# Sine tables, square-root table load, last-pair casts, one stage-3 product and fillers placed elsewhere in a spectral-filter and MLP kernel

## Chip, cores, metric

One core of one Trainium2 chip. The metric is the device time of the kernel in microseconds; medians of repeated executions are given with their number.

## The reference, cut

```python
x = A_x                                             # 1 x 2048 x 512, bf16
X = rfft2(layernorm(x)) * (w_r + 1j * w_i)
h = x + irfft2(X)                                   # first half
r = relu(layernorm(h) @ w1 + b1)                    # 512 -> 1792
out = h + (r * r) @ w2 + b2                         # 1792 -> 512, second half
```

The kernel computes the transforms as matmuls with cosine and sine tables made on the chip. Frequencies are handled in eight pairs (0 to 7): stage 2 (tile U), stage 3 (X, or AB which VectorE turns into X), the product with W (mA, mB, Z, M on VectorE), stage 4 (into T2). The last stage ("s5", "s6") turns T2 into h for one of 16 row groups at a time; the MLP follows in five chunks.

## The kernel before: what the change and the argument touch

In the timelines each engine's instructions stand in the order in which the program lists them (ScalarE before: sine tables at 44.27 and 45.23 us, cast of pair 5 at 45.75, table load at 46.80, cast of pair 6 at 48.30), so an early item of a queue delays the later ones.

```python
def warm(o, n):                                     # fillers: nobody reads the result
    for _ in range(n):
        nc.tensor.matmul(o, lhsT=ones[:, 0:P], rhs=ones[:], start=True, stop=True)

ps = tc.alloc_tile_pool(name="ps", bufs=4, space=PSUM)       # 4 tiles of two banks
def mm_tile(name, dt=FP32):
    return ps.tile([P, 4096 // size(dt)], dt, tag="mm", name=name)
...
def stage4(pr, split=False):
    Z, M = Zs.pop(pr), Ms.pop(pr, None)
    pts = [mm_tile("p4a"), mm_tile("p4b")] if split else [mm_tile("p4")] * 2
    if split:                                       # pair 7
        for u, tb in (...):
            for lt in (1, 0, 3, 2):
                r, e = lt // 2, lt % 2
                nc.tensor.matmul(pts[r][:, 256 * lt:256 * lt + 256], lhsT=M[:, u, r, e::2], rhs=tb,
                                 start=(u == 0 and e == 1), stop=(u == 1 and e == 0))
    ...                                             # other pairs: one tile
    if split:
        nc.scalar.copy(dst[:, 0:2], src[0][:, 0:2])          # the two halves of T2 for pair 7
        nc.vector.tensor_copy(dst[:, 2:4], src[1][:, 2:4])
    else:
        nc.scalar.copy(dst, src[0])
...
for pr in range(9):
    if pr == 1:
        stage3(3)
    if pr + 3 < 8:
        stage2(pr + 3)
    if 1 < pr and pr + 2 < 8:
        stage3(pr + 2)
    if pr == 7:
        warm(mm_tile("idle")[:, 0:512], 3)
    if pr > 0:
        stage4(pr - 1, split=(pr == 8))
    if pr == 8:
        warm(mm_tile("idle")[:, 0:512], 3)
    if pr < 8:
        spectral(pr)                                # VectorE
    if pr == 5:
        sin_of(GI...)                               # sine tables of the last stage, ScalarE
        nc.scalar.activation(GIn..., ACT.Sin, scale=-SIN_SCALE)
    if pr == 6:
        nc.scalar.activation(junk1[:], eps[:], ACT.Sqrt, bias=eps[:])   # loads the Sqrt table
ps.release()
ps = ctx.enter_context(tc.tile_pool(name="ps2", bufs=3, space=PSUM))    # tiles of one bank
...
def s5_first(g):                                    # first products of the last stage
    two = [bank("p5o", "ph", 3), bank("p5", "pp", 3)]
    for e in range(2):                              # even l, then odd l
        for r in range(2):
            nc.tensor.matmul(two[e][:, 0:256], lhsT=T2[:, 2 * r + e, g]..., rhs=GI[:, 2 * r + e, :], ...)
...
s5_first(0); s5_whole(1); s5b(0); s6(0); s6(1)
rest = [s5(2, True), s5(3, True)]
s6a(1); s6b(0, True); s6b(1)                        # h and its statistics
warm(idle[:], 11)
...                                                 # u of groups 0 and 1, transposes, UT, MLP
```

## Time and profile before

| | before |
|---|---|
| median of the first 3 runs | 172.66 us (172.52 to 172.68) |
| span of the profiled run | 170.8 us |
| TensorE (PE) busy | 157.6 us, 92% |
| VectorE (DVE) / ScalarE (ACT) busy | 123.6 us / 106.3 us |
| granted TensorE clock (1.00 is full speed) | 1.00 |
| first MLP matmul | 56.66 us into the span |

TensorE's 92% also holds the fillers. PEld is TensorE's weight load. "idle before" stands in square brackets at the end of a timeline line, with the instruction that ended it.

### The profile page before, as it was taken

What the parts mean: (1) busy time and instruction counts of PE and PEld (TensorE: products, weight loads), DVE (VectorE), ACT (ScalarE), POOL (GpSimd) and SP (SyncE); (2) the same over time, 40 slices, a digit from 0 to 9 for tenths busy, and PEclk for the clock granted to TensorE, in tenths of its full rate; (3) what the DMA queues carried; (4) which work ended last, traced back from release to release, by engine and by line L of the source; (5) the groups of instructions that cost most, each with busy time, mean ns of one, the idle gap of its engine ahead of it and who ended that gap; (6) DMA issues with size and microseconds to landing.
All of it is one profiled execution on the core that took longest, in us unless ns stands there. A gap on an engine that the chain in (4) does not pass through costs nothing.

```text
span 170.8 us, 2709 instructions
## 1 busy us (share of the span) xinstructions
PE 157.6 (92%) x967; PEld 92.4 (54%) x981; DVE 123.6 (72%) x287; ACT 106.3 (62%) x188; POOL 36.7 (22%) x63
## 2 busy tenths in 40 slices
PE   3988797999989899899999999999999999999992
PEld 1455565887854774456445444544544454556461
DVE  6998678979956698668997577498567577578320
ACT  3999785898976772288653677245387434478200
POOL 7788900000000003134000235000034200025000
PEclk9999999999999999999999999999999999999999
DMA  5994999992000000100000100000100001010011
GB/s 165 326 281 83 223 152 272 387 241 26 0 0 0 4 0 2 55 12 0 0 31 31 35 0 2 0 31 31 35 30 0 0 31 33 25 38 0 0 60 34
DMA packets 12621, 11.42 MB, mean 67 GB/s; under 512 B 6976, under 2 KB 11072, under 8 KB 12608
## 3 DMA queue, kind: packets, MB, share of 16 engines
q1 hardware_dynamic: 12448, 10.33, 22.6%
q0 software_dynamic: 160, 0.92, 1.9%
q8 instruction: 7, 0.11, 0.3%
q14 instruction: 6, 0.05, 0.1%
HBM read 8.01 MB, written 2.10 MB: 59 GB/s over the span
## 4 chain that ended last, share of the span: by engine, by line
PE 72%; DVE 16%; ACT 5%; issue 2%; POOL 2%; DVEq 0%; POOLq 0%; ACTq 0%
PE ph L688 29%; PE po L721 25%; DVE st L215 3%; PE p L542 3%; PE p L344 3%; ACT U L361 2%; PE po L709 2%; PE p L643 2%; PE p L587 1%; PE idle L259 1%; POOL rs L222 1%; DVE KFr L226 1%; DVE mA L419 1%; ACT X L391 1%; DVE mB L419 1%
## 5 line engine op out<-in xcount | busy, mean ns | idle before, releaser
L688 PE MATMUL ph<-UT,W 128*128 128x384 bf16 (+2 forms) x278 | 49.8, 336 | 1.6 <-DVE UT L774 0.6
L691 ACT ACTIVATE rl<-ph,b1f 128x384 bf16<-128x384 f32 (+2 forms) x70 | 41.5, 602 | 13.7 <-PE ph L688 10.6
L721 PE MATMUL po<-W,act 128*128 128x512 bf16 x203 | 48.1, 379 | 0.4
L692 DVE TENSOR_TENSOR act<-rl 128x384 bf16<-128x384 bf16 (+2 forms) x70 | 34.2, 514 | 15.4 <-ACT rl L691 14.9
L688 PEld LDWEIGHTS <-W 128*128 128x128 bf16 x280 | 27.3, 98 | 22.9 <-issue 2.1
L695 POOL TENSOR_TENSOR hb<-hs,b2b 128x512 f32<-128x512 bf16 x16 | 18.4, 1153 | 98.2 <-DVE act L692 98.2
L721 PEld LDWEIGHTS <-act 128*128 128x128 bf16 x210 | 20.4, 98 | 21.8
L725 DVE TENSOR_TENSOR ot<-po,hb 128x512 bf16<-128x512 f32 x15 | 10.3, 688 | 9.3 <-PE po L721 8.0
L591 DVE SCALAR_TENSOR_TENSOR hs<-p,xs 128x512 bf16<-128x512 f32 x15 | 10.3, 684 | 1.2 <-PE p L587 0.9
L259 PE MATMUL p<-ones 128*128 128x512 bf16 x22 | 8.1, 516 | 2.9 <-POOL ones L152 2.9
L546 ACT COPY od<-p 128x256 f32<-128x256 f32 x14 | 5.1, 370 | 7.9 <-PE p L542 7.9
L647 ACT COPY UT<-p 128x768 bf16<-128x768 bf16 (+1 forms) x4 | 3.6, 906 | 9.4 <-PE p L643 9.4
L542 PE MATMUL p<-GI,T 128*128 128x256 bf16 x56 | 8.2, 272 | 0.4 <-DVE hs L591 0.2
L259 PEld LDWEIGHTS <-ones 128*128 128x128 bf16 x40 | 4.4, 112 | 7.6 <-POOL ones L152 2.9
L602 ACT ACTIVATE junk<-hs 128x512 bf16<-128x512 bf16 x6 | 3.8, 630 | 7.6 <-DVE hs L591 7.6
L344 PE MATMUL p<-GF,Bt 128*128 128x256 bf16 x64 | 8.3, 273 | 0.0
L577 DVE TENSOR_TENSOR R<-p,od 128x256 bf16<-128x256 f32 x15 | 6.2, 415 | 2.4 <-ACT od L561 1.3
L215 DVE BATCH_NORM_STATS2 st<-xs 128x6 f32<-128x512 bf16 x12 | 7.8, 676 | 0.0
L542 PEld LDWEIGHTS <-T 128*128 128x128 bf16 x56 | 5.4, 97 | 3.5 <-issue 1.2
L473 ACT CAST T<-p 128x1024 bf16<-128x1024 f32 x7 | 7.2, 1025 | 0.0
L344 PEld LDWEIGHTS <-Bt 128*128 128x128 bf16 x64 | 6.1, 98 | 1.4 <-DVE Bt L251 0.4
L605 DVE BATCH_NORM_STATS2 st<-hs 128x6 f32<-128x512 bf16 x9 | 6.3, 695 | 0.3
(177 smaller groups left out, 226.0 us busy)
## 6 DMA issues: line engine op xcount, KB each, us to landing
W<-in_B_w_dram SPq DMA_DIRECT2D x2, 1792.0 KB, 10.3
out_dram<-ot SPq DMA_DIRECT2D x15, 128.0 KB, 1.8
xs<-in_A_x_dram SPq DMA_DIRECT2D x3, 512.0 KB, 6.5
WB<-in_A_w_r_dram SPq DMA_DIRECT2D x1, 578.2 KB, 6.0
WB<-in_A_w_i_dram SPq DMA_DIRECT2D x1, 578.2 KB, 7.2
xs<-in_A_x_dram SPq DMA_DIRECT2D x2, 256.0 KB, 3.3
b2b<-in_B_b_dram SPq DMA_DIRECT2D x1, 128.0 KB, 8.7
out_dram<-ot SPq DMA_DIRECT2D x2, 64.0 KB, 1.9
```

The lines of the kernel that those rows point to most:

```text
L215: nc.vector.bn_stats(st[:], xs[:, g, :])
L259: nc.tensor.matmul(o, lhsT=ones[:, 0:P], rhs=ones[:], start=True, stop=True)
L344: nc.tensor.matmul(puv[:, :, e, :], lhsT=Bt[:, 2 * t + 1 - e, 2 * pr + q, :], rhs=GFv[:, t, :, e, :], start=(t == 0), stop=(t == 1))
L473: nc.scalar.copy(dst, src[0])
L542: nc.tensor.matmul(pe[:, 256 - 256 * e:512 - 256 * e], lhsT=T2[:, lt, g].rearrange("p q s -> p (q s)"), rhs=GI[:, lt, :], start=(r == 0), ...
L591: nc.vector.scalar_tensor_tensor(hs[:, g, :], Ys.pop(g)[:], WSC, xs[:, g, :], ALU.mult, ALU.add)
L688: nc.tensor.matmul(ph[:, 0:n], lhsT=W1[:, d, bass.ts(f, P)], rhs=UT[:, d, 0:n], start=(d == 0), stop=(d == ND - 1))
L691: nc.scalar.activation(rl[:, 0:n], ph[:, 0:n], ACT.Relu, bias=b1f[:, f:f + 1], scale=1.0)
L692: sq = nc.vector.tensor_tensor(act[:, f, 0:n], rl[:, 0:n], rl[:, 0:n], ALU.mult)
L695: add = nc.gpsimd.tensor_tensor(hb[:, g, :], hs[:, g, :], b2b[:], ALU.add)
L721: nc.tensor.matmul(po[:], lhsT=act[:, f, bass.ts(i, P)], rhs=W2[:, f, :], start=(f == 0), stop=(f == NF - 1))
L725: nc.vector.tensor_tensor(ot[:], po[:], hb[:, g, :], ALU.add)
```

## The change

Intent: take ScalarE's sine tables and table load out of the stretch ahead of the last pair's casts, let the last stage begin on half of the last pair, remove a wait of VectorE for pair 5, and drop fillers that outlast what they cover.

```diff
-                for lt in (1, 0, 3, 2):
+                for lt in (0, 2, 1, 3):
                     r, e = lt // 2, lt % 2
-                    nc.tensor.matmul(pts[r][:, 256 * lt:256 * lt + 256], lhsT=M[:, u, r, e::2], rhs=tb,
-                                     start=(u == 0 and e == 1), stop=(u == 1 and e == 0))
+                    nc.tensor.matmul(pts[e][:, 256 * lt:256 * lt + 256], lhsT=M[:, u, r, e::2], rhs=tb,
+                                     start=(u == 0), stop=(u == 1))
@@ casts of the last pair
-            nc.scalar.copy(dst[:, 0:2], src[0][:, 0:2])
-            nc.vector.tensor_copy(dst[:, 2:4], src[1][:, 2:4])
+            nc.scalar.copy(dst[:, 0::2], src[0][:, 0::2])
+            nc.vector.tensor_copy(dst[:, 1::2], src[1][:, 1::2])
@@ loop over the pairs
+        if pr == 3:
+            stage3(5)
         if pr + 3 < 8:
             stage2(pr + 3)
-        if 1 < pr and pr + 2 < 8:
+        if pr == 0:
+            sin_of(GI[:]..., fiI[:])
+        if pr == 2:
+            nc.scalar.activation(GIn[:], fiI[:]..., ACT.Sin, scale=-SIN_SCALE)
+        if pr in (2, 4, 5):
             stage3(pr + 2)
-        if pr == 7:
-            warm(mm_tile("idle")[:, 0:512], 3)
@@ end of the loop
         if pr == 5:
-            sin_of(GI[:]..., fiI[:])
-            nc.scalar.activation(GIn[:], fiI[:]..., ACT.Sin, scale=-SIN_SCALE)
             nc.gpsimd.tensor_copy(b1f[:], b1b[:])
-        if pr == 6:
             nc.scalar.activation(junk1[:], eps[:], ACT.Sqrt, bias=eps[:])
@@ ahead of the MLP
-    warm(idle[:], 11)
+    warm(idle[:], 7)
```

More of the change, by code (lines that the diff above doesn't have):

```diff
@@ L496 @@
             stage3(3)
+        if pr == 3:
+            stage3(5)
         if pr + 3 < 8:
             stage2(pr + 3)
-        if 1 < pr and pr + 2 < 8:
+        if pr == 0:
+            sin_of(GI[:].rearrange("p t c -> p (t c)"), fiI[:])
+        if pr == 2:
+            nc.scalar.activation(GIn[:], fiI[:].bitcast(I16)[:, ::2].rearrange("p (t c) -> p t c", t=4)[:, 0::2, :],
+                                 ACT.Sin, scale=-SIN_SCALE)
+        if pr in (2, 4, 5):
             stage3(pr + 2)
-        if pr == 7:
-            warm(mm_tile("idle")[:, 0:512], 3)
         if pr > 0:
@@ L511 @@
         if pr == 5:
-            sin_of(GI[:].rearrange("p t c -> p (t c)"), fiI[:])
-            nc.scalar.activation(GIn[:], fiI[:].bitcast(I16)[:, ::2].rearrange("p (t c) -> p t c", t=4)[:, 0::2, :],
-                                 ACT.Sin, scale=-SIN_SCALE)
             nc.gpsimd.tensor_copy(b1f[:], b1b[:])
-        if pr == 6:
             nc.scalar.activation(junk1[:], eps[:], ACT.Sqrt, bias=eps[:])
```

## The prediction

> **What bounds the kernel now.** I read the page first (time per engine, the slices, the chain that ended last), then the table by stretches, then the timelines of ScalarE (ACT), VectorE (DVE) and TensorE (PE) from 23 to 61 us, the part the change touches.
>
> ```profile
> core 0: us, PE busy (x) PEld busy (x) DVE busy (x) ACT busy (x) POOL busy (x), PEclk, DMA share, GB/s
> ...
> 29.00:45.00 16.00, 15.78 (x131) 12.34 (x133) 14.63 (x34) 13.78 (x16) 0.37 (x1) 1.00 0.67 196
> 45.00:50.00 5.00, 4.17 (x31) 2.82 (x31) 3.52 (x8) 4.75 (x7) 0.00 (x0) 1.00 0.00 0
> 50.00:57.00 7.00, 6.25 (x45) 3.87 (x45) 3.99 (x12) 4.18 (x11) 0.00 (x0) 1.00 0.00 0
> 57.00:72.00 15.00, 14.04 (x103) 9.44 (x102) 12.68 (x36) 7.46 (x18) 2.27 (x2) 1.00 0.03 10
> 72.00:165.00 93.00, 92.22 (x504) 47.78 (x511) 63.73 (x129) 52.89 (x100) 16.13 (x14) 1.00 0.06 19
> ```
>
> PE is busy 92.22 of the 93 us from 72 to 165, and nearly all of 57 to 72. So this MLP part is a block of fixed length: whatever moves its first matmul (L688, at 56.66) moves the end by the same. From 29 to 45 PE is full too, with useful work. The loose part is 45 to 57, where PE's "busy" holds fillers. There the waits decide. First ScalarE:
>
> ```profile
> 44.27 1.09 ACT L124 ACTIVATE GI<-fiI 128x1024 bf16<-128x1024 int16 x1
> 45.23 0.65 ACT L513 ACTIVATE GIn<-fiI 128x512 bf16<-128x512 int16 x1
> 45.75 1.03 ACT L473 CAST T<-p 128x1024 bf16<-128x1024 f32 x1
> 46.80 1.28 ACT L517 ACT_TABLE_LOAD   x1
> 48.09 0.29 ACT L517 ACTIVATE junk<-eps 128x1 f32<-128x1 f32 x1
> 48.30 0.99 ACT L473 CAST T<-p 128x1024 bf16<-128x1024 f32 x1
> 49.19 0.59 ACT L470 CAST T<-p4a 128x512 bf16<-128x512 f32 x1
> ```
>
> The cast of pair 6 starts at 48.30, behind sine tables, pair 5 and the table load; the half cast of pair 7 follows at 49.19 and ends at 49.78. The next lines are PE around it:
>
> ```profile
> 45.45 1.91 PE L463 MATMUL p<-EI,Z 128*128 128x256 bf16 x16
> 47.72 0.39 PE L446 MATMUL p4a<-EI,M 128*128 128x256 bf16 x2 [0.36 <-DVE M L434]
> ...
> 48.38 0.38 PE L446 MATMUL p4b<-EI,M 128*128 128x256 bf16 x2
> 48.60 0.81 PE L259 MATMUL idle<-ones 128*128 128x512 bf16 x3
> 49.83 0.39 PE L558 MATMUL p5o<-GI,T 128*128 128x256 bf16 x2 [0.42 <-ACT T L470]
> ...
> 53.29 2.32 PE L259 MATMUL idle<-ones 128*128 128x512 bf16 x10
> 55.45 0.61 PE L773 MATMUL p<-ident,u 128*128 128x128 bf16 x8
> 56.66 1.47 PE L688 MATMUL ph<-UT,W 128*128 128x256 bf16 x12 [0.61 <-DVE UT L774]
> ```
>
> Pair 7's products start at 47.72, released by DVE; the last stage's first matmul (49.83) is released by that late ScalarE cast, although VectorE's half (48.80 plus 0.69) was ready at 49.49. Then the transposes L773 start at 55.45 with no wait shown: they stand behind the 11 fillers (one record of them is missing). Their input was ready earlier, as VectorE's line shows:
>
> ```profile
> 54.18 0.41 DVE L769 TENSOR_SCALAR u<-hs,mv,rs 128x512 bf16<-128x512 bf16 x1
> ...
> 54.70 0.41 DVE L769 TENSOR_SCALAR u<-hs,mv,rs 128x512 bf16<-128x512 bf16 x1
> 56.09 0.42 DVE L774 COPY UT<-p 128x512 bf16<-128x512 bf16 x1 [0.98 <-PE p L773]
> ```
>
> The second u is done at 55.11, so the fillers are late for it.
>
> **What the Trainium skill says.** "ScalarE: Activation LUTs", section What ACT_TABLE_LOAD costs, gives 1283 ns for the load plus a drain of some 1380 ns. The trace agrees with the load (1.28 us), but the next ACTIVATE starts 1.29 us after the load did: no such drain is seen beyond the wait for the cast before it, so I count 1.28. The same section says ACTIVATEs one after another overlap by about 93 ns; here casts of 1.02 us start 0.91 apart (36.37, 37.27, 38.18), so I count pitches, not durations. "TensorE: Matmul & The Clock Gate", Part 1, says that an idle window of about 3.4 us halves the clock. The change leaves PE gaps of 1.1 us at most (below), and before has one of 1.15 us at 29.12 with a granted clock of 1.00: no drop is expected. "PSUM — Partial Sum Buffer", section PSUM bank collisions raise a hardware error, asks that two engines not read one bank at once; the even and odd halves still lie in two tiles, as the old halves did, so both casts can still run side by side.
>
> **The change, part by part.**
>
> **Sine tables.** GI (1.09) goes behind the cast of U of pair 3 (28.05 to 29.06). ScalarE idles 1.11 us there, until 30.18. GI would run 28.97 to 30.06: just fits. GIn (0.65, a pitch of 0.56) goes behind U of pair 5 (starts 32.92), ahead of an idle of 0.60 that ends at 34.55: 33.83 to 34.48, fits. Cost: 0. Removed from 44.27 to 45.75: about 1.48 us.
>
> **Table load.** It moves ahead of pair 5's cast: pair 4 ends at 44.40, load 44.42 to 45.70, junk to 46.0, pair 5's cast 45.92 to 46.9 (0.17 later than before, nobody waits for it). Pair 6's products are no longer held up by three fillers (3 x 0.215 = 0.65), so they run 44.80 to 46.54 instead of 45.45 to 47.19; they need Z of pair 6, ready at 44.68. Pair 6's cast: 46.83 to 47.85, before pair 7's products exist. So ScalarE is free for pair 7.
>
> **Stage 3 of pair 5.** Today DVE waits 0.87 us at 38.35 for AB of that pair. Its cast moves one pitch up (37.27 to 36.37), so that wait goes nearly wholly. But it is given back. X of pair 6 is cast at 40.65, set by a PE that streams without a gap from 29.12 to 44.80, and is ready at 41.70 where DVE now reaches it at 41.47. AB of pair 7 comes two ScalarE pitches later (40.65, 41.56, 42.46) plus 1.03, ready at 43.53; DVE, 0.67 early, stands there and starts at 43.53 instead of 43.58. So M of pair 7 comes only 0.05 us earlier: pair 7's products start at 47.67. Worth: 0.05.
>
> **Last pair by even and odd.** Products 47.67 to 48.55, the even tile complete after the sixth. From the before trace: a tile's reader starts 0.31 us after its last 256-wide matmul starts (48.49 to 48.80). Even: 48.23 + 0.31 = 48.54, ScalarE 0.59, done 49.13. Odd: 48.75, VectorE 0.69, done 49.44. Three fillers end at 49.20. The even products of the last stage's first group need the even half alone: 49.20 (before 49.83, so 0.63 sooner). The odd ones wait for 49.44 and start at 49.49 (before 50.06, so 0.57 sooner). The whole group behind them: 49.71 instead of 50.28, 0.57 sooner. That 0.57 passes through the PSUM copy, the residual sum, the statistics and the norm (od, R, hs, bn, u: all waits on one another, nothing else in the way): u of group 1 ends at 54.54 instead of 55.11, that of group 0 at 54.02.
>
> **Fewer fillers.** The two s5 groups end at 52.50 instead of 53.07. Eleven fillers would end at 52.50 + 11 x 0.2155 = 54.87; seven end at 54.01, when u of group 0 is just there. Transposes of group 0 at 54.10, of group 1 at 54.62 (wait for u). Group 1's tile is complete 0.38 us after its first transpose (4 x 0.055 less one, plus 0.22), so VectorE copies from 55.04 to 55.46 (before 56.09 to 56.51) and the first L688 starts 0.15 later, at 55.61.
>
> **Sum.** 56.66 - 55.61 = 1.05 us: 0.57 from the casts and 0.48 from fillers that were no longer hidden. The MLP behind it is full PE, so the end moves by it: 172.66 - 1.05 = **171.6 us**.
>
> **The rivals.** (1) The strided halves are tracked as overlapping, so VectorE's cast waits for ScalarE's, or the even products for both. Against it: today VectorE's cast of pair 7 (48.80) runs beside ScalarE's of pair 6 (48.30 to 49.28), whose targets interleave in T2. If only the even products wait for both, the gain falls by 0.2, to 171.85; if the casts run one behind the other (VectorE 49.2 to 49.9), the first part is lost and only fillers are won: 172.2. (2) The 0.87 us wait removed for pair 5 is not given back: M of pair 7 would come up to 0.8 sooner, the end at 170.8. Against it: ScalarE's order and PE's full stretch. (3) GI does not fit (a slack of 0.02 to 0.1) and pushes AB of pair 3 and what follows. ScalarE has idles of 0.5 to 0.6 us ahead, and PE's buffers are read over a microsecond before they are needed again, so a slip of 0.1 to 0.3 is swallowed; at worst 171.9. (4) The gap of 1.1 us on PE (46.54 to 47.67) and the shorter warm-up lower the clock: PE at half speed for some 3 us, 174 or more. The clock of 1.00 through the gap at 29.12 speaks against it.
>
> **Range and chances.** Steps of 0.05 to 0.1 are uncertain in a chain of ten waits, rival 1 in its mild form pulls up, rival 2 down: 171.2 to 172.05. A gain of over 2% needs 3.45 us, over three times what the loose stretch offers; a loss of 2% needs the clock drop. Chances 0.01, 0.98, 0.01.
>
> **What would show it.** Right: GI near 28.97 and GIn near 33.83 with no later AB or X; the table load at 44.4; the even products at 49.2 and the odd at 49.5; DVE waiting for X of pair 6 and AB of pair 7 (some 0.2 and 0.6 us) in place of 0.87 for AB of pair 5; M of pair 7 still near 47.2; transposes near 54.1 and 54.6; first L688 near 55.6; and from there to the end as long as before, 114.1 us of span. Wrong: pair 7's products starting before 47.4, VectorE's cast waiting for ScalarE's, or a granted clock below 1.00.

## The result

| | median | span of the profiled run | first MLP matmul |
|---|---|---|---|
| before, 4 runs beside the change | 172.67 us (172.52 to 172.93) | 170.8 us | 56.66 us |
| after, 4 runs | 171.79 us (171.78 to 171.90) | 170.0 us | 55.90 us |

The ratio is 0.9949, 95% interval 0.9932 to 0.9966: faster by half a per cent, inside 2%. The prediction was 171.6, range 171.2 to 172.05.

Lines of the changed kernel answer to those of before; line numbers from the loop on are one higher (L688 is now L689). The table by stretches:

```profile
core 0: us, PE busy (x) PEld busy (x) DVE busy (x) ACT busy (x) POOL busy (x), PEclk, DMA share, GB/s
29.00:45.00 16.00, 15.90 (x134) 12.43 (x134) 14.79 (x35) 15.25 (x18) 0.26 (x1) 1.00 0.66 194
45.00:50.00 5.00, 3.82 (x32) 2.69 (x29) 3.47 (x7) 3.38 (x5) 0.00 (x0) 1.00 0.00 0
72.00:165.00 93.00, 92.65 (x515) 48.10 (x513) 63.88 (x129) 52.79 (x100) 16.11 (x14) 1.00 0.05 18
```

ScalarE took the sine tables into 29 to 45 (15.25 us busy instead of 13.78) without slowing TensorE there, and is freer from 45 to 50 (3.38 instead of 4.75). The MLP is as full as it was. The last output sum starts at 166.76 instead of 167.53, 0.77 us sooner, and the first MLP matmul 0.76 us sooner: from that matmul on nothing changed. Now ScalarE's timeline ahead of it:

```profile
44.41 1.28 ACT L518 ACT_TABLE_LOAD   x1
45.70 0.29 ACT L518 ACTIVATE junk<-eps 128x1 f32<-128x1 f32 x1
45.90 1.91 ACT L473 CAST T<-p 128x1024 bf16<-128x1024 f32 x2
48.51 0.58 ACT L470 CAST T<-p4a 128x512 bf16<-128x512 f32 x1 [0.70 <-PE p4a L446]
```

The casts of pairs 5 and 6 are over at 47.81, and ScalarE waits 0.70 us for pair 7's products instead of being late for them. Its half is done at 49.09 instead of 49.78. TensorE's timeline:

```profile
47.64 0.39 PE L446 MATMUL p4a<-EI,M 128*128 128x256 bf16 x2 [0.95 <-DVE M L434]
...
49.56 0.38 PE L559 MATMUL p5o<-GI,T 128*128 128x256 bf16 x2 [0.23 <-DVE T L471]
49.78 0.38 PE L559 MATMUL p<-GI,T 128*128 128x256 bf16 x2
...
52.79 1.67 PE L259 MATMUL idle<-ones 128*128 128x512 bf16 x7
54.37 0.92 PE L774 MATMUL p<-ident,u 128*128 128x128 bf16 x8
55.90 1.47 PE L689 MATMUL ph<-UT,W 128*128 128x256 bf16 x12 [0.61 <-DVE UT L775]
```

The first even products start at 49.56 and not at 49.20: they wait for VectorE's half (L471, over at 49.42), of which they read nothing. That is the one place where the prediction's chain did not hold. VectorE's timeline:

```profile
41.67 0.70 DVE L419 TENSOR_TENSOR mA<-X,WB 128x1024 bf16<-128x1024 bf16 x1 [0.16 <-ACT X L391]
...
43.50 0.42 DVE L409 TENSOR_TENSOR X<-AB 128x512 bf16<-128x512 bf16 x1 [0.53 <-ACT AB L400]
...
47.16 0.42 DVE L434 TENSOR_TENSOR M<-Z 128x512 bf16<-128x512 bf16 x1
```

The wait of 0.87 us for pair 5 is gone and 0.69 us of it has come back as two other waits; M of pair 7 comes 0.08 us sooner.

### The profile page after: what moved, and what is told of

The parts are those of the page before. It is cut to its first block, busy times and chain, and to the rows that moved or that the text cites. A ratio compares the mean times of both kernels' runs of the same rounds, so it can differ in the third digit from the quotient of the medians.

```text
span 170.0 us, 2709 instructions
## 1 busy us (share of the span) xinstructions
PE 156.7 (92%) x974; PEld 91.6 (54%) x974; DVE 123.6 (73%) x287; ACT 106.4 (63%) x188; POOL 36.5 (21%) x63
## 3 DMA queue, kind: packets, MB, share of 16 engines
HBM read 8.01 MB, written 2.10 MB: 59 GB/s over the span
## 4 chain that ended last, share of the span: by engine, by line
PE 74%; DVE 14%; ACT 5%; POOL 2%; issue 2%; DVEq 0%; POOLq 0%
PE ph L689 29%; PE po L722 25%; PE p L344 4%; DVE st L215 3%; PE p L543 3%; PE po L710 2%; PE p L644 2%; PE p L588 1%; POOL rs L222 1%; ACT U L361 1%; DVE KFr L226 1%; DVE hs L592 1%; ACT X L391 1%; PE p L383 1%; DVE fiE L181 1%
## 5 line engine op out<-in xcount | busy, mean ns | idle before, releaser
L689 PE MATMUL ph<-UT,W 128*128 128x384 bf16 (+2 forms) x280 | 50.0, 336 | 1.5 <-DVE UT L775 0.6
L722 PE MATMUL po<-W,act 128*128 128x512 bf16 x210 | 49.1, 379 | 0.0
L689 PEld LDWEIGHTS <-W 128*128 128x128 bf16 x280 | 27.3, 98 | 22.9 <-issue 2.1
L259 PE MATMUL p<-ones 128*128 128x512 bf16 x23 | 7.6, 482 | 2.9 <-POOL ones L152 2.9
L259 PEld LDWEIGHTS <-ones 128*128 128x128 bf16 x33 | 3.6, 113 | 6.9 <-POOL ones L152 2.9
L244 PE MATMUL p<-KFr,xs 128*128 128x256 bf16 x24 | 5.5, 273 | 1.1 <-DVE KFr L226 1.1
```

The lines of the kernel that those rows point to most:

```text
L689: nc.tensor.matmul(ph[:, 0:n], lhsT=W1[:, d, bass.ts(f, P)], rhs=UT[:, d, 0:n], start=(d == 0), stop=(d == ND - 1))
L722: nc.tensor.matmul(po[:], lhsT=act[:, f, bass.ts(i, P)], rhs=W2[:, f, :], start=(f == 0), stop=(f == NF - 1))
```

## The experiments

Twelve kernels ran; all gave correct results. The profiled executions differ in when x lands: VectorE's first fold of a statistic into a table (KFr) starts between 7.42 and 8.01 us, in the latest of them behind a wait of 0.48 us for x's DMA, and everything behind is shifted by that. So I compare the distance from that fold to the first MLP matmul, read from the timelines of each run:

| kernel | median us (runs) | ratio to before | first fold | first MLP matmul | distance |
|---|---|---|---|---|---|
| before | 172.67 (4) | 1 | 7.43 | 56.66 | 49.23 |
| after | 171.79 (4) | 0.9949 | 7.42 | 55.90 | 48.48 |
| acts_alone | 172.36 (6) | 0.9980 | 7.43 | 56.45 | 49.02 |
| fillers_alone | 172.21 (6) | 0.9973 | 7.42 | 56.15 | 48.73 |
| no_evenodd | 171.86 (6) | 0.9953 | 7.43 | 55.90 | 48.47 |
| stage3_back | 171.93 (6) | 0.9953 | 7.51 | 56.05 | 48.54 |
| pair7_ahead | 171.35 (5) | 0.9921 | 7.61 | 55.47 | 47.86 |
| four_pools | 171.61 (5) | 0.9941 | 7.62 | 55.86 | 48.24 |
| four_pools_no_evenodd | 171.74 (5) | 0.9945 | 7.86 | 56.21 | 48.35 |
| four_pools_pair7 | 170.93 (4) | 0.9899 | 8.01 | 55.63 | 47.62 |
| no_fillers | 172.85 (6, in two groups) | 0.9999 | 7.42 | 55.80 | 48.38 |
| one_pool, and two like it | 219.2 to 219.8 (6 each) | 1.27 | | | |

The ratios' 95% intervals are about 0.0015 wide to either side, so times alone separate the larger steps only; the distances separate the small ones. Each distance comes from one execution. As a check, the fastest run of each kernel of the first eleven rows, set against after's fastest (171.78 us), differs from it as the distance does to within 0.03 us, so steps of a few hundredths of a us are not resolved.

**acts_alone.** The kernel before, with only this moved:

```diff
+        if pr == 0:
+            sin_of(GI[:]..., fiI[:])
+        if pr == 2:
+            nc.scalar.activation(GIn[:], fiI[:]..., ACT.Sin, scale=-SIN_SCALE)
         if 1 < pr and pr + 2 < 8:
             stage3(pr + 2)
@@
         if pr == 5:
-            sin_of(GI...); nc.scalar.activation(GIn...)
             nc.gpsimd.tensor_copy(b1f[:], b1b[:])
-        if pr == 6:
             nc.scalar.activation(junk1[:], eps[:], ACT.Sqrt, bias=eps[:])
```

> The kernel before with only ScalarE's sine tables and table load moved. Theory (the casts' share and the fillers' share are two separate terms): pair 6's cast starts near 47.4 instead of 48.30, so pair 7's ScalarE half ends near 49.2 and VectorE's half (49.49) becomes the last; the last stage's first product starts near 49.63 instead of 49.83, and the 11 fillers, still there, move with it and hide the rest: some 0.20 us faster than before, 172.45. Rival (late casts were the whole loss): 0.7 us or more faster, below 172.0.

Pair 6's cast starts at 47.39, the first product of the last stage at 49.63, and the distance is 0.21 us shorter, as the theory said. It is not the whole loss: the eleven fillers still stand behind.

**fillers_alone.** The kernel before, with `warm(..., 3)` at `pr == 7` removed and eleven fillers cut to seven.

> The kernel before with only the fillers cut (three of pair 7 gone, eleven down to seven). Theory: the casts stay late (first product of the last stage at 49.83), but the transposes start near 54.65 and 55.18 instead of 55.45, the first MLP product at 56.17 instead of 56.66: 0.49 us faster than before, 172.2. Rival (fillers cost nothing or keep the clock up): no change, or slower with a granted clock under 1.00.

The first product stays at 49.81, the transposes start at 54.62, the distance is 0.50 us shorter. So the two terms are separate and add up: 0.21 and 0.50 are 0.71 of the change's 0.75.

**no_evenodd.** The changed kernel with the last pair's casts as before:

```diff
-                for lt in (0, 2, 1, 3):        # and pts[e], dst[:, 0::2] / dst[:, 1::2]
+                for lt in (1, 0, 3, 2):        # and pts[r], dst[:, 0:2] / dst[:, 2:4]
```

> The changed kernel with the last pair cast in the old halves (l 0 and 1 by ScalarE, 2 and 3 by VectorE). Theory (the first product of the last stage waits for both casts, whatever the halves): the same as the changed kernel within 0.1 us, 171.8, first product again near 49.56. Rival (the prediction: the even half lets the first products go ahead of VectorE's cast): slower than the changed kernel by 0.2 us or more.

48.47 against 48.48: in the changed kernel the even and odd halves gain nothing. The first product again starts at 49.57 behind VectorE's cast.

**stage3_back.** The changed kernel with stage 3 of pair 5 behind stage 2 of pair 6:

```diff
-        if pr == 3:
-            stage3(5)
...
-        if pr in (2, 4, 5):
+        if pr in (2, 3, 4, 5):
             stage3(pr + 2)
```

> The changed kernel with stage 3 of pair 5 in its old place, behind stage 2 of pair 6. Theory (the wait of 0.87 us is given back at the tables of pairs 6 and 7): VectorE waits 0.9 us for AB of pair 5 again, its waits for X of pair 6 and AB of pair 7 are gone, M of pair 7 comes 0.05 later, time 171.85. Rival (the move is worth its wait): 0.6 to 0.9 us slower, 172.4 to 172.7.

VectorE waits 0.88 us for AB of pair 5 again, and the waits for X of pair 6 and AB of pair 7 are gone from its timeline. The distance is 0.06 us longer. The move is worth those 0.06, not the wait that it removes.

**one_pool, one_pool_no_evenodd, both: the pool handover, first try.** Why do the even products wait for a cast that they do not read? Two reasons were left: the interleaved halves of T2 are tracked as overlapping, or something else ties them. The compiled program of the changed kernel has, ahead of the first weight load of the last stage, waits for VectorE's last cast, for ScalarE's last cast, and, on the first matmul, for the fillers of pair 7, though the product's bank is none of theirs. These are the last users of the first PSUM pool. To test it, all PSUM was made one pool that is never released:

```diff
-    ps = tc.alloc_tile_pool(name="ps", bufs=4, space=PSUM)
+    ps = ctx.enter_context(tc.tile_pool(name="ps", bufs=1, space=PSUM))
+    bk = [ps.tile([P, 1024], FP32, name=f"bk{i}") for i in range(4)]
     def mm_tile(name):
+        return bk[...]                             # the tile that the pool gave before
@@
-    ps.release()
-    ps = ctx.enter_context(tc.tile_pool(name="ps2", bufs=3, space=PSUM))
@@ bank()
+        return bk[i // 2][:, 512 * (i % 2):512 * (i % 2) + 512]   # the bank that it gave before
```

> The changed kernel with all PSUM tiles cut out of four tiles of one pool, same banks, so that no second pool is opened on the memory of the first. Theory (the first product of the last stage waits for both casts because it is the first user of the second PSUM pool, which waits for the last users of the first; not because the halves overlap): the even products start near 49.2, as soon as ScalarE's half is there, the odd ones near 49.5; everything behind comes 0.3 us sooner, 171.5. Rival (the interleaved halves of T2 are tracked as overlapping): the first product still starts at 49.5 behind VectorE's cast, 171.8.

> The same one pool with the last pair cast in the old halves. Theory: the first product (l 0) starts near 49.2, the second (l 2) must wait for VectorE's cast, 49.5; so the group behind starts 0.1 us later than with even and odd: 171.6, slower than one pool with even and odd by 0.1 us. Rival (even and odd is what gains, 0.3): 171.8.

> The changed kernel with one PSUM pool and stage 3 of pair 7 ahead. Theory (two separate terms): the sum of both, 0.55 and 0.3, gives 170.95; the even products start near 48.6, when the three fillers end. Rival (they are the same term): 171.2.

The times were far off all three expectations: 219.77, 219.22 and 219.22 us. One timeline of one_pool shows why, and it also answers the question that was asked:

```profile
49.54 0.69 DVE L475 CAST T<-bk 128x512 bf16<-128x512 f32 x1 [0.88 <-PE bk L450]
49.89 0.13 PEld L564 LDWEIGHTS <-T 128*128 128x128 bf16 x2 [0.30 <-ACT T L474]
49.92 0.76 PE L564 MATMUL bk<-GI,T 128*128 128x256 bf16 x4
50.28 0.11 PEld L564 LDWEIGHTS <-T 128*128 128x128 bf16 x2 [0.27 <-DVE T L475]
...
52.23 0.38 PE L589 MATMUL bk<-xs,identW 128*128 128x512 bf16 x1 [0.67 <-ACT R L578]
```

The even products (49.92) now go ahead of VectorE's cast, which ends at 50.23; only the odd ones' weights wait for it. So the halves of T2 are not the tie. But L589 waits 0.67 us for a ScalarE cast that reads the other bank of the same two-bank tile, which it need not. With two banks in one tile, waits come all through the MLP (the matmuls of L694 wait 15.5 us for ScalarE's L697; in after all idle time before that line's matmuls is 1.5 us). My edit had changed more than it was to change.

**four_pools.** The repair: the same banks, but four pools of two banks released one by one, then eight pools of one bank.

```diff
-    ps = tc.alloc_tile_pool(name="ps", bufs=4, space=PSUM)
+    pss = [tc.alloc_tile_pool(name=f"ps{i}", bufs=1, space=PSUM) for i in range(4)]
     def mm_tile(name):
+        return pss[...].tile([P, 1024], FP32, tag="mm", name=name)
@@
-    ps.release()
-    ps = ctx.enter_context(tc.tile_pool(name="ps2", bufs=3, space=PSUM))
+    for q in reversed(pss):
+        q.release()
+    banks = [ctx.enter_context(tc.tile_pool(name=f"bk{i}", bufs=1, space=PSUM)) for i in range(8)]
@@ bank()
+        return banks[i].tile([P, 2048 // size(dt)], dt, tag="b", name=name)
```

> The changed kernel with PSUM as four pools of two banks (same banks), each followed by pools of one bank, instead of one pool handed over whole. In the one-pool runs the even products did go ahead of VectorE's cast (49.92, cast's end 50.23), but a matmul into one bank of a two-bank tile then waited for readers of its other bank, which cost 47 us; here each bank is a tile of its own again. Theory (the handover of the pool is what holds the even products): even products near 49.18, odd near 49.5, the whole group behind near 49.72 instead of 50.00, 0.28 us faster than the changed kernel: 171.5. Rival (the gain is lost further on, or many small pools cost waits elsewhere): 171.8 or more.

This profiled run is 0.20 us late from the start (fold at 7.62). Its timeline:

```profile
48.72 0.59 ACT L473 CAST T<-p4a 128x512 bf16<-128x512 f32 x1 [0.70 <-PE p4a L449]
48.94 0.69 DVE L474 CAST T<-p4b 128x512 bf16<-128x512 f32 x1 [0.81 <-PE p4b L449]
49.36 0.13 PEld L565 LDWEIGHTS <-T 128*128 128x128 bf16 x2 [0.30 <-ACT T L473]
49.39 0.38 PE L565 MATMUL p5o<-GI,T 128*128 128x256 bf16 x2
49.68 0.11 PEld L565 LDWEIGHTS <-T 128*128 128x128 bf16 x2 [0.20 <-DVE T L474]
```

The even products start at 49.39, 49.19 without the late start: the predicted 49.20. VectorE's cast ends 0.24 us later, at 49.63. The group behind starts at 49.92 (L576), so 0.28 us sooner than after's 50.00, and the distance is 0.24 us shorter. The handover of the pool held the even products; nothing else was changed, down to the banks (compiled, the 974 matmuls of both kernels write the same PSUM addresses in the same order).

**four_pools_no_evenodd.** The old halves on the four pools.

> The same four pools with the last pair cast in the old halves. Theory: the first product (l 0) near 49.18, the second (l 2) held to 49.5 by VectorE's cast, the whole group near 49.83: even and odd are worth 0.11 us here, so 171.6. Rival (even and odd is the whole 0.3): 171.8.

48.35 against 48.24: with the handover out of the way even and odd is worth 0.11 us, as expected.

**pair7_ahead.** The changed kernel, and stage 3 of pair 7 one place ahead as well:

```diff
-        if pr in (2, 4, 5):
+        if pr in (2, 4):
             stage3(pr + 2)
+        if pr == 4:
+            stage3(7)
```

> The changed kernel with stage 3 of pair 7 one place ahead too, before stage 4 of pair 3. Theory (the wait removed for pair 5 is given back at AB of pair 7, which stands one ScalarE cast behind where it could): AB of pair 7 is cast near 41.5 instead of 42.44, VectorE's wait of 0.53 us there goes, M of pair 7 comes near 46.6 instead of 47.16, pair 7's products near 47.05, and as the casts of pair 6 and 7 follow at once, the end comes 0.55 us sooner: 171.2. Rival (something else holds pair 7, for instance ScalarE's table load or pair 6's cast): 171.6 or more.

ScalarE's timeline now has AB of pair 7 (L400) directly behind X of pair 6 (this run is 0.19 us late from the start):

```profile
40.82 1.01 ACT L391 CAST X<-p 128x1024 bf16<-128x1024 f32 x1 [0.50 <-PE p L389]
41.73 1.02 ACT L400 CAST AB<-p 128x1024 bf16<-128x1024 f32 x1
42.63 1.95 ACT L473 CAST T<-p 128x1024 bf16<-128x1024 f32 x2
```

VectorE uses it at 43.09 with no wait, M of pair 7 starts at 46.73, and the distance is 0.62 us shorter. So what gave back pair 5's wait was pair 7's place in ScalarE's queue.

**four_pools_pair7.** Both.

> Four pools and stage 3 of pair 7 one place ahead. Stage 3 alone gave 0.43 us in the trace (pair 7's products 47.21 instead of 47.64). Theory (separate terms): even products near 48.75 (the three fillers end there), 0.28 + 0.43 = 0.71 us faster than the changed kernel: 171.1, the fastest of all. Rival (same term): 171.35.

The distance is 47.62: 0.86 shorter than after, the sum of 0.24 and 0.62. Three of four runs took 170.91 to 170.93 us; the fourth, the profiled one, 171.55, has the late x (fold at 8.01). It is the fastest kernel, 0.9899 of before (0.9885 to 0.9914).

**no_fillers.** The changed kernel without the ten fillers left in this stretch (`warm(..., 3)` at `pr == 8` and `warm(idle[:], 7)`).

> The changed kernel without its last ten fillers (three behind pair 7, seven ahead of the transposes). Theory (nobody waits for them any more, and gaps of 1.1 and 1.6 us on TensorE don't lower its clock): 171.8 within 0.1, granted clock 1.00. Rival (the fillers keep the clock up): matmuls behind the gaps run slower, granted clock under 1.00, 172.5 or more.

My theory fell. The first MLP matmul came 0.10 us sooner, but two runs took 171.68 and 171.72 us with a granted clock of 1.00, and four took 172.85 to 173.70 with 0.99. Tables by stretches of the profiled run (172.85) show where:

```profile
52.00:56.00 4.00, 1.86 (x18) 1.19 (x17) 3.34 (x11) 2.89 (x9) 0.00 (x0) 1.00 0.00 0
...
52.85:56.26 3.41, 1.27 (x14) 0.89 (x14) 2.81 (x10) 2.07 (x7) 0.00 (x0) 1.00 0.00 0
56.26:59.67 3.41, 3.41 (x18) 2.20 (x16) 1.69 (x7) 1.65 (x4) 0.00 (x0) 0.50 0.02 5
```

From 52 to 56 TensorE was busy for 1.86 of 4 us (1.00 is the clock, the third number from the end), and from 56.26 to 59.67, when the MLP had begun, its clock was 0.50. The same stretch of the changed kernel:

```profile
52.00:56.00 4.00, 3.27 (x25) 1.86 (x24) 3.25 (x10) 2.98 (x9) 0.00 (x0) 1.00 0.00 0
```

3.27 of 4 us, and no fall. The longest gap of no_fillers was 1.41 us; the prediction had argued from a gap of 1.15 us alone.

The traces' records of the clock tell more: it changes only at the ends of intervals of 3.41 us, one after another. In the fourteen traces, eleven intervals ran at half clock, some of them behind the last matmul; each followed an interval in which TensorE was busy for at most 1.38 us (here 1.27, from 52.85 to 56.26), and the 691 others, each behind 1.57 us or more, ran at full clock. So the busy time of one interval tells the falls apart; the longest gap in it does not (1.41 us here, but 1.78 without a fall in one_pool, from 177.37 to 180.79). The first interval starts between 5.72 and 8.64 us into the span, at another place in each run, so it is chance whether the thin stretch falls into one interval. That fits the two runs of six without a fall, but only one of the six was profiled. The interval that fell is where the seven fillers had stood. An estimate for the three: no stretch of 3.41 us of this trace around their place has less than 1.68 us busy, so they should not be needed for the clock. That, and how few of the seven would do, was not run.

## Why the prediction was right, and its one failed step

**Bound.** Right: the MLP is a block. From its first matmul to the last output sum it is 110.87 us before and 110.86 after.

**Sine tables and table load.** Right: GI ran from 28.94, GIn from 33.80, X of pair 4 at 34.53 and AB of pair 3 at 30.16 were not later, the load stood at 44.41. The rival that GI does not fit is out.

**Stage 3 of pair 5.** Right in mechanism and size: waits of 0.16 and 0.53 us (predicted about 0.2 and 0.6) came in place of 0.87; stage3_back puts it at 0.06 us (predicted 0.05), and pair7_ahead shows the cause by removing it, for 0.62 us. The rival that the wait is won is out.

**Last pair by even and odd.** This is the failed step: "The even products of the last stage's first group need the even half alone: 49.20". They started at 49.56, when VectorE's half was there. The term of 0.57 us was 0.27 us (49.83 to 49.56). ScalarE's earlier casts give 0.20 of it (acts_alone, 49.63); the rest goes with M of pair 7, which comes 0.08 us sooner. The new halves give nothing: no_evenodd differs by 0.01. The outcome was named as the mild form of rival 1, with 171.85 us, but for a reason that was wrong: the halves in T2 are tracked apart (one_pool, four_pools). The even products are the first to use the second PSUM pool, and that waits for the last readers of the first. I had read the data dependences and not the handover of the memory.

**Fewer fillers.** Right: 0.48 predicted, 0.50 measured alone. But the support for the clock was too weak. I argued from the longest gap, and no_fillers shows that a stretch with gaps of at most 1.41 us can lose the clock. Seven fillers were enough in every run here (mean granted clock 0.996 or more; one fall gives 0.99); the argument given would have allowed dropping all of them. "TensorE: Matmul & The Clock Gate", Part 1, speaks of a window of activity of 3.4 us that runs freely. The traces agree: the clock changes only at the ends of intervals of 3.41 us, which begin at another place in each run.

**Sum.** 0.27 and 0.49 make the 0.76 us of the trace. The medians differ by 0.88, the fastest runs of each by 0.74; the rest is the scatter of before. That the medians come nearer to the predicted 1.05 than the trace does is luck; the sum was 0.29 us too large.

## What to carry to other kernels

Before counting on a part of a result being enough to start, look at what else the first user waits for: a memory pool handed over whole made the first user wait for all its last users (0.24 us here), and smaller pools let it go. A wait removed in a queue pays only as far as the next item of the same queue is not late itself, so follow the item to its last reader and move the last one of the queue too. Fillers are judged by two things, when they end and how full they keep the engine in each interval of its clock (3.41 us here); cut them to the first without losing the second.

## What the Trainium skill lacked or had wrong

- "TensorE: Matmul & The Clock Gate", table under "Why this matters for your kernels", advises against idle gaps of more than about 3 us between bursts of matmuls. Here the clock was lost with gaps of at most 1.41 us (0.50 for 3.41 us in the profiled run; four of six runs of no_fillers have a mean clock of 0.99). Part 1's activity window is the better guide, but a busy time that holds the clock is not given: in these traces 1.38 of 3.41 us or less lost it and 1.57 or more kept it.
- "ScalarE: Activation LUTs", What ACT_TABLE_LOAD costs, counts a drain of some 1380 ns to each switch. The load took 1.28 us as stated, it began 0.02 to 0.03 us after the cast before it had ended, and the next ACTIVATE started 1.29 us after the load's start both before (46.80 to 48.09) and after (44.41 to 45.70): no such drain shows.
- No page that I read says that opening a PSUM pool on a released one makes its first matmul wait for all last users of the old pool: 0.24 us of distance here (four_pools), nor that a matmul into one bank of a two-bank tile is made to wait for a reader of the other bank: 0.67 us in one place, 47 us over the kernel with all that follows (one_pool).
